# A fused attention, expert and softplus kernel: float64 conversion with one operand in PSUM, expert shares through ScalarE, input sums on GpSimd

## The chip, the cores and the metric

The kernel runs on one NeuronCore of a Trainium2 chip. The metric is the device time of one execution in microseconds (us); lower is better. Five engines work side by side, each with its own in-order queue: TensorE (PE, matrix products into PSUM), VectorE (DVE), ScalarE (ACT), GpSimd (POOL) and SyncE (SP), which only starts DMA transfers here. ACT starts a few transfers as well.

## The reference

Three stages follow each other. Shapes: q, k, v are (4, 8, 576, 64); the tokens that come out are 2304 rows of 512.

```
# 1 attention on keys and values averaged over groups of 8
k_p, v_p = mean of k, v over 8 neighbours           # 72 positions
x = softmax(q @ k_p.T / 8) @ v_p                    # -> x (2304, 512)
# 2 eight experts, every token goes to all of them
P = exp(x @ w_gate - max); 8 times: normalise rows, then columns; P *= N / E
out = sum over e of P[:, e] * (relu(x @ w1[e]) @ w2[e])   # w1 (8,512,1024)
# 3 softplus layer
out = softplus(out @ w_in) @ w_out                  # w_in (512,2048), w_out (2048,512)
```

The weights `w_in` and `w_out` of stage 3 arrive as float64, so the kernel has to turn 64-bit numbers into float32 on the chip, with integer operations on their two 32-bit words. All other inputs are float32.

## The kernel before

**Precision.** Each float32 product is done as three products of rounded halves: hi*hi, lo*hi, hi*lo, where hi is the value rounded to TensorE's format and lo the remainder. So every operand needs a `hi` (a copy by ACT) and a `lo` (a subtraction by POOL for weights, by DVE for most activations). `three` (line 791) issues the three matmuls.

**Phases and units.** The tokens are three groups ("pairs") of 768. `phases` (line 160) lists six phases: the expert layer on groups 0, 1, 2 (f = 0, 1, 2) and the softplus layer on groups 1, 2, 0 (f = 3, 4, 5). An expert phase has 32 units u (8 experts times 4 slices of 256 hidden columns), a softplus phase 8. A unit has a first part (x times w1, or w_in) and a second part (hidden times w2, or w_out). The list `todo` puts the first part of unit u+1 ahead of the second part of unit u.

**Fewer products.** The first part of every unit does a 2x2 block product with seven block products instead of eight; it needs four sums of input blocks, called t1 to t4, and remainders (lo) of the seven inputs, which are prepared during the phase before and parked in DRAM (`xlod`). In the two "block phases" f = 1 and 2 (`TWICE`) the second part is done the same way over pairs of units: the second part of an even unit has two form products, that of an odd unit has five, and the results are collected in seven matrices m1 to m7, which `joined` (line 1140) later adds up on POOL to the group's output.

**Side work.** What isn't part of the current unit is cut into small steps. `side` is a list of steps, with None for an empty slot; `hook` (line 1304) takes the next entry. Hooks stand between the products of a first part and after the tiles of a second part. If `side` is empty and the slot is marked light, `hook` calls `convert` instead. In the block phases hooks run in odd units only (`between`, line 1540); a chunk of conversion starts at k = 0 of an odd unit only if `side` is empty, and then goes on at each k. `ahead` (line 1484) fills `side` with the next phase's input sums and remainders: after unit 20 in f = 0, unit 2 in f = 1, unit 10 in f = 2. In f = 2 the seven joins of group 1 run by themselves from unit 0 on, two in each even unit (list `joins`).

**The conversion.** `from_float64` (line 1219) is a generator with six steps for each of 32 chunks of 128x512 numbers. `raw` holds a chunk's words in SBUF (tile `f`), `a` is a PSUM bank (`da`), `t` an SBUF tile (`dt`). Its DVE instructions stand on lines 1245, 1247, 1250, 1252, 1254, 1256 and 1257; line 1248 is one on ACT (absolute value). Line 1250 is the only one with both operands in SBUF:

```
ts(dn, dn, 1, None, op0=ALU.logical_shift_right)        # L1250: SBUF -> SBUF
```

In the same step as the last of them SP's store of the chunk (line 1258) and the load of the next chunk into the same raw buffer (line 1259) are issued. Two raw buffers exist until unit 26 of f = 0, one afterwards. `needed` forces chunks that a weight load is about to read.

**PSUM.** In f = 0 and the softplus phases there are four banks for first parts, three ("y") for second parts and one ("c") for side work. In the block phases PSUM is two sets (L, R) of double banks, each rotating by two.

**Shares.** In f = 0 the results of the first four experts are collected without their share P. Once P is known, `shares_to_raw` (line 1325) multiplies them in: for expert 0 one ACT instruction per tile, for the others one DVE instruction per tile that reads two SBUF tiles (line 1334), 18 in all.

Of the kernel before, what the change touches and what calls it, by code (L numbers as in the profile page):

```python
# [11 lines left out]
U32 = mybir.dt.uint32  # L12
# [7 lines left out]
def attention_moe_softplus_kernel(  # L20
# [637 lines left out]
    xs_next = {}  # L658
    spare = ["y"]

    def t_sums_banked(x, t):

        for o, a, b in (
            (t(0), block(x, 0, 1), block(x, 0, 0)), (t(2), block(x, 1, 1), block(x, 0, 1)),
            (t(1), block(x, 1, 1), t(0)), (t(3), block(x, 1, 0), t(1)),
        ):
            for c in range(2):
                got = []

                def copy(a=a, c=c, got=got):  # L670
                    got.append(bank("xs", spare[0])[:, :a.shape[2]])
                    nc.scalar.copy(got[0], a[:, c, :])

                def subtract(o=o, b=b, c=c, got=got):
                    nc.vector.tensor_tensor(o[:, c, :], got.pop(), b[:, c, :], op=ALU.subtract)

                yield copy
                yield subtract
# [67 lines left out]
    def sums_with_remainders(f, x, t, joins=()):  # L746

        parts = moe_parts(x, t)
        of = {name: q for q, (name, _) in enumerate(parts)}
        b = lambda i, j: block(x, i, j)  # L750
        ops = [
            *joins,
            (lambda: pool_sub(t(0), b(0, 1), b(0, 0)), "t1"),
            (lambda: pool_sub(t(2), b(1, 1), b(0, 1)), "t3"),
            (lambda: pool_sub(t(1), b(1, 1), t(0)), "t2"),
            (lambda: pool_sub(t(3), b(1, 0), t(1)), "t4"),
        ]
        ready = [] if joins else ["b11", "b21", "b22"]
        steps = []
        lag = [None, None]  # L760
        since = EVERY
        while ops or any(lag) or ready or steps:
            if (ops or any(lag)) and since >= EVERY:
                op, name = ops.pop(0) if ops else (None, None)
                lag.append(name)
                due = lag.pop(0)
                ready.extend([due] if due else [])
                since = 0
                if op:
                    yield op  # L770
                continue
            since += 1
            if not steps and ready:
                q = of[ready.pop(0)]
                steps = [*remainder(f, q, parts[q][1]), None]
            yield steps.pop(0) if steps else None
# [438 lines left out]

    f64_t = []
    converted = [0]

    def from_float64():

        ts, stt = nc.vector.tensor_scalar, nc.vector.scalar_tensor_tensor
        every = list(widths())
        unread = list(enumerate(every))
        loaded = []

        def fetch(at):
            if unread and at < len(f64_t):
                i, (src, _) = unread.pop(0)
                _, c, f, w = src.shape
                raw = f64_t[at].rearrange("p (c f w) -> p c f w", c=c, w=w)  # L1230
                nc.sync.dma_start(raw, src)
                loaded.append((i, at, raw))

        for at in range(len(f64_t)):
            fetch(at)
        for _ in range(4):
            yield True
        while loaded:
            i, at, raw = loaded.pop(0)
            up = raw[:, :, :, 1].rearrange("p c f -> p (c f)")  # L1240
            dn = raw[:, :, :, 0].rearrange("p c f -> p (c f)")
            size = lambda x: x.bitcast(F32)
            a = bank("da", "c", U32)
            t = tpool.tile([P, up.shape[1]], F32, tag="ex", name="dt")
            ts(a, up, 3, 0x3FFFFFF8, op0=ALU.logical_shift_left, op1=ALU.bitwise_and)
            yield False
            stt(a, up, 0xC0000000, a, op0=ALU.bitwise_and, op1=ALU.bitwise_or)
            nc.scalar.activation(size(up), size(up), AF.Abs)
            yield False
            ts(dn, dn, 1, None, op0=ALU.logical_shift_right)  # L1250
            yield False
            stt(t, size(up), 1.125 * 2.0 ** -15, size(a), op0=ALU.is_ge, op1=ALU.mult)
            yield False
            ts(a, t.bitcast(U32), 0xFF800000, None, op0=ALU.bitwise_and)
            yield False
            stt(size(a), dn, 2.0 ** -51, size(a), op0=ALU.mult, op1=ALU.mult)
            nc.vector.tensor_tensor(t, t, size(a), op=ALU.add)
            nc.sync.dma_start(every[i][1].rearrange("p c f -> p (c f)"), t)
            fetch(at)
            converted[0] += 1  # L1260
            yield True


    conversion = from_float64()
    between_chunks = [True]

    def convert():
        if converting[0] is not None:
            between_chunks[0] = next(conversion, None)
            if between_chunks[0] is None:  # L1270
                between_chunks[0] = True
                converting[0] = None

    def needed(chunks):
        while converted[0] < chunks:
# [49 lines left out]
    def shares_to_raw(experts):  # L1325

        for e in experts:
            for i in range(TP0 // P):
                def add(i=i, e=e):
                    a, s = acc_of(1, i), prob[:, i, e:e + 1]  # L1330
                    if e == 0:
                        nc.scalar.activation(a, a, AF.Copy, scale=s)
                    else:
                        nc.vector.scalar_tensor_tensor(a, raw_of(e, i), s, a, op0=ALU.mult, op1=ALU.add)
                side.extend([add, None, None] if e else [add])

    def load_x(pair):
        o = OFF[pair] - TP0
# [144 lines left out]

    def ahead(f, kind, u):

        if f + 1 == len(phases) or u != (20 if f == 0 else 10 if f == TWICE[-1] else 2 if kind == "moe" else 0):
            return
        nkind, npair = phases[f + 1]
        x, t = x_for(f + 1), t_in(t_at[f + 1], npair)
        if kind == "sp":  # L1490
            joins = ()
            if npair in TWICE:
                joins = joined(npair)
            else:
                for i in range(PAIRS[npair] // P):
                    side.extend([lambda i=i: turn(i, npair, 1), None])
            side.extend(sums_with_remainders(f + 1, x, t, joins))
            if joins:
                side.append(lambda: nc.sync.dma_start(g_t[1], gd))
            return  # L1500
        if nkind == "moe":
            side.append(lambda: load_x(npair))
            side.extend([None] * (8 if f == 0 else 5))
        if f == 0:
            for i, y in enumerate(t_sums_banked(x, t)):
                side.extend([y, None] if i % 2 else [y])
            for i, y in enumerate(remainders(f + 1, x, t)):
                side.extend([y, None] if i % 3 == 2 else [y])
            return
        side.extend(in_sixes(t_sums_banked(x, t), 2))  # L1510
        side.extend(in_sixes(remainders(f + 1, x, t), 3))

    joins = []

    for step, (what, n) in enumerate(todo):
# [3 lines left out]
        if what == "first":  # L1519
# [10 lines left out]
            if twice(n):  # L1530
                if not twice(n - 1):
                    while not between_chunks[0]:
                        convert()
                    open_banks("right", ("R", 2))
                    open_extra(
                        ("hhi", [P, 2 * TB], F32R), ("hlo", [P, 2 * TB], F32R), ("whi", [P, UC * HALF], F32R),
                        ("wlo", [P, UC * HALF], F32R), ("a21", [P, 2, TB], F32), ("s3", [P, 2, TB], F32),
                    )

                def between(k):  # L1540

                    if to_split and k in (1, 3, 4, 5):
                        to_split.pop(0)()
                    if u % 2 == 0:
                        if joins and k in (1, 4):
                            joins.pop(0)[0]()
                        return
                    if k == 0:
                        sharing[0] = not side
                    if not sharing[0]:  # L1550
                        hook()
                    elif k == 0 or not between_chunks[0]:
                        convert()

                away[0] = "LR"[u // 2 % 2]
# [36 lines left out]
        else:  # L1592
            if twice(n):
                second_twice(n)
                if f == TWICE[-1] and u == 0:
                    joins.extend(joined(TWICE[0]))
                if u == NU1 - 1 and not twice(n + 1):
                    assert not joins
                    open_extra(("xl", [P, 2 * TB], F32))
# [12 lines left out]
            for i in range(PAIRS[pair] // P):  # L1612
# [22 lines left out]
                    while more_stores:  # L1635
                        more_stores.pop(0)()
                if kind == "moe" or i >= 3:
                    hook(i >= (2 if f == 1 else 3))
            del h_t[n], w2_t[n]
            while pending:  # L1640
                pending.pop(0)()
# [43 lines left out]
```

## Time and profile before

| | us |
|---|---|
| median of 3 runs | 2017.49 |
| lowest and highest | 2008.28 and 2017.8 |
| the profiled execution's own time | 2014.24 |
| its span, first to last instruction | 2012.1 |

| engine | busy us | share of the span |
|---|---|---|
| PE (products) | 1953.7 | 97% |
| DVE | 1498.8 | 74% |
| POOL | 1472.0 | 73% |
| ACT | 971.0 | 48% |

The busy time of PE is modelled and its matmuls overlap, so a busy PE is not PE at its best pace. The chain that ended last is PE for 81% of the span and DVE for 9%. In a row of waits the first name is who waited, then for whom, then the total time, the number of waits and the longest. A row of the chain has a start, a length and what ran.

### The profile page before, as it was taken

The page shows a single profiled execution, that of the slowest core. Times are in us where ns is not written, and L with a number is a line of the kernel's source. Part 1 is how long each engine was busy: PE and PEld are TensorE (multiplying, and loading weights), DVE is VectorE, ACT ScalarE, POOL GpSimd, SP SyncE. Part 2 cuts the span into 40 slices and gives each one's busy share as a digit, 9 for nine tenths or more (in the row PEclk, how much of TensorE's full clock was granted, in tenths as well). Part 3 has the DMA queues.
Part 4 walks back from the last instruction along what each step waited for, and adds up shares of the span by engine and source line. Part 5 has one row for each costly group of instructions (what it writes and reads, how often), then busy time and mean ns, then how long its engine had stood idle before and what let it go on. Part 6 is the DMA issues. An engine that isn't in the chain of part 4 may idle for free.

```text
span 2012.1 us, 30503 instructions
## 1 busy us (share of the span) xinstructions
PE 1953.7 (97%) x10954; PEld 1804.6 (90%) x10954; DVE 1498.8 (74%) x2355; ACT 971.0 (48%) x1773; POOL 1472.0 (73%) x1134
## 2 busy tenths in 40 slices
PE   9899999999999999999999989999999989999999
PEld 7687788888988999999999889899999988888987
DVE  6775577887677777878888779888788866646455
ACT  6545334333334645554545544355554555655543
POOL 6776668777777777777777787677787868666553
PEclk9999999999999999999999999999999999999999
DMA  7444334555556654555555545444555532523411
GB/s 201 121 150 144 124 110 151 174 185 178 185 166 244 185 172 143 159 162 155 170 165 181 170 150 161 139 155 152 178 148 162 175 107 97 189 105 110 148 63 63
DMA packets 213347, 306.56 MB, mean 152 GB/s; under 512 B 33308, under 2 KB 147532, under 8 KB 212940
## 3 DMA queue, kind: packets, MB, share of 16 engines
q1 hardware_dynamic: 203116, 290.85, 45.9%
q10 hardware_dynamic: 10080, 13.77, 1.9%
q8 instruction: 86, 1.41, 0.3%
q14 instruction: 65, 0.53, 0.1%
HBM read 239.30 MB, written 65.27 MB: 151 GB/s over the span
## 4 chain that ended last, share of the span: by engine, by line
PE 81%; DVE 9%; POOL 3%; DMA 3%; issue 3%; ACT 1%; SPq 0%; DVEq 0%; ACTq 0%; POOLq 0%
PE py L794 42%; PE p L794 36%; DVE p L843 1%; DVE a L842 1%; POOL w1lo L289 1%; POOL w2lo L289 1%; DVE u L842 1%; PE px L522 1%; PE s L477 1%; PE pa L512 0%; DVE g L1126 0%; DMA xlod<-xl 0%; DMA f<-in_moe_w_out_dram 0%; DVE p L1039 0%; ACT w1hi L320 0%
## 5 line engine op out<-in xcount | busy, mean ns | idle before, releaser
L794 PE MATMUL p<-xhi,w1hi 128*128 128x384 f32 x1680 | 572.5, 341 | 19.6 <-DVE u L842 8.3
L794 PE MATMUL p<-xlo,w1hi 128*128 128x384 f32 x1680 | 565.1, 336 | 3.8 <-DMA xlo<-xlod 3.7
L794 PE MATMUL p<-xhi,w1lo 128*128 128x384 f32 x1680 | 565.8, 337 | 0.0
L289 POOL TENSOR_TENSOR w2lo<-w2raw,w2hi 128x512 fp32r<-128x512 f32 (+1 forms) x235 | 367.5, 1579 | 132.4 <-ACT w2hi L243 119.3
L289 POOL TENSOR_TENSOR w1lo<-w1raw,w1hi 128x512 fp32r<-128x512 f32 x240 | 239.6, 1021 | 248.4 <-ACT w1hi L320 248.3
L794 PEld LDWEIGHTS p<-xhi,w1hi 128*128 128x128 f32 x1680 | 316.5, 188 | 36.7 <-DVE u L842 9.2
L794 PEld LDWEIGHTS p<-xlo,w1hi 128*128 128x128 f32 x1680 | 316.8, 189 | 8.7 <-DMA xlo<-xlod 4.0
L794 PEld LDWEIGHTS p<-xhi,w1lo 128*128 128x128 f32 x1680 | 316.6, 188 | 0.0
L289 POOL TENSOR_TENSOR w1lo<-sums,w1hi 128x1024 fp32r<-128x1024 f32 x120 | 289.1, 2410 | 2.0 <-ACT w1hi L320 2.0
L794 PE MATMUL py<-w2hi,hhi 128*128 128x512 f32 x672 | 271.3, 404 | 9.0 <-DVE g L1126 7.2
L794 PE MATMUL py<-w2lo,hhi 128*128 128x512 f32 x672 | 266.3, 396 | 0.0
L794 PE MATMUL py<-w2hi,hlo 128*128 128x512 f32 x672 | 266.1, 396 | 0.0
L794 PE MATMUL py<-hhi,w2hi 128*128 128x384 f32 x716 | 245.8, 343 | 8.4 <-DVE a L842 8.4
L794 PE MATMUL py<-hhi,w2lo 128*128 128x384 f32 x716 | 242.1, 338 | 1.5 <-POOL w2lo L289 1.4
L794 PE MATMUL py<-hlo,w2hi 128*128 128x384 f32 x716 | 242.1, 338 | 0.0
L842 DVE TENSOR_TENSOR g<-py,g 128x768 f32<-128x768 f32 x210 | 199.7, 951 | 52.7 <-PE py L794 52.7
L886 ACT CAST hhi<-p 128x768 fp32r<-128x768 f32 x128 | 102.7, 802 | 249.3 <-DVE p L883 208.6
L794 PEld LDWEIGHTS py<-w2hi,hhi 128*128 128x128 f32 x672 | 126.7, 189 | 41.2 <-DVE g L1126 9.9
L794 PEld LDWEIGHTS py<-w2hi,hlo 128*128 128x128 f32 x672 | 126.6, 188 | 31.3
L794 PEld LDWEIGHTS py<-hhi,w2hi 128*128 128x128 f32 x716 | 135.3, 189 | 19.2 <-DVE a L842 16.1
L794 PEld LDWEIGHTS py<-w2lo,hhi 128*128 128x128 f32 x672 | 127.0, 189 | 24.4
L794 PEld LDWEIGHTS py<-hhi,w2lo 128*128 128x128 f32 x716 | 135.3, 189 | 2.4 <-POOL w2lo L289 2.4
(161 smaller groups left out, 3565.1 us busy)
## 6 DMA issues: line engine op xcount, KB each, us to landing
w1raw<-in_moe_w_dram SPq DMA_DIRECT2D x96, 512.0 KB
w2raw<-td SPq DMA_DIRECT2D x128, 256.0 KB
sums<-sd SPq DMA_DIRECT2D x62, 512.0 KB
w2raw<-in_moe_w_dram SPq DMA_DIRECT2D x96, 256.0 KB
w2raw<-in_moe_w_dram SPq DMA_DIRECT2D x32, 512.0 KB
sd<-sums SPq DMA_DIRECT2D x32, 512.0 KB
td<-w2raw SPq DMA_DIRECT2D x64, 256.0 KB
xlo<-xlod SPq DMA_DIRECT2D x35, 384.0 KB
```

Of the source, the lines that this page charges most:

```text
L289: nc.gpsimd.tensor_tensor(o, a, b, op=ALU.subtract)
L477: nc.tensor.matmul(ps[:QP, j * 2 * SP:(j + 1) * 2 * SP], qT[:, j * QP:(j + 1) * QP], kb)
L522: nc.tensor.matmul(px[h * D:(h + 1) * D, :W], vp[:, h, :], aT[:, h, :])
L794: nc.tensor.matmul(ps, lhs[a], rhs[b], start=first and i == 0, stop=last and i == 2, skip_group_check=goes_on,)
L842: vadd = lambda o, x, y: nc.vector.tensor_tensor(o, x, y, op=ALU.add)
L843: vsub = lambda o, x, y: nc.vector.tensor_tensor(o, x, y, op=ALU.subtract)
L886: nc.scalar.copy(h_slot(q)[0], src)
```

## The change

Four things change.

1. Conversion. The bank `a` takes over what `t` held and the other way round, and the shift of the low word (line 1250) no longer works in place in SBUF but writes to a PSUM bank `r`: in the block phases the second half of the same double bank, elsewhere a bank from the three of the second part. Every DVE instruction of a chunk now has exactly one operand in PSUM (or reads SBUF and writes PSUM).
2. Store and next load of a chunk are put off (`settle`): in the block phases to k = 2 of the following even unit; elsewhere to the next call of `convert`, after which 3 calls (two raw buffers) or 10 calls (one buffer) pass before the next chunk starts. No chunk starts in unit 31 of a block phase. In f = 0 the third tile of a second part becomes a light slot too.
3. Shares. For experts 1 to 3 ACT scales the raw tile into a "y" bank and, a hook later, DVE adds that bank to the sum.
4. Input sums of the phases 2 and 3 (f + 1 when f is 1 or 2) are done by four POOL instructions of 128x768 instead of sixteen steps by ACT and DVE through a bank. They run from unit 0 on in even units, at k = 1 and 4, behind `load_x` (f = 1) or the seven joins (f = 2); then `side` gets the remainders.

```diff
+    def t_sums(x, t):
+        b = lambda i, j: block(x, i, j)
+        return [
+            (lambda: pool_sub(t(0), b(0, 1), b(0, 0)), "t1"),
+            (lambda: pool_sub(t(2), b(1, 1), b(0, 1)), "t3"),
+            (lambda: pool_sub(t(1), b(1, 1), t(0)), "t2"),
+            (lambda: pool_sub(t(3), b(1, 0), t(1)), "t4"),
+        ]
...
-            a = bank("da", "c", U32)
+            in_c = "c" in banks
+            if in_c:
+                a = bank("da", "c", U32)
+            else:
+                both = banks[away[0]].tile([P, 2, 512], U32, tag=f"two{away[0]}", name="da")
+                a, r = both[:, 0], both[:, 1]
...
-            ts(dn, dn, 1, None, op0=ALU.logical_shift_right)
+            if not in_c:
+                ts(r, dn, 1, None, op0=ALU.logical_shift_right)
             yield False
-            stt(t, size(up), 1.125 * 2.0 ** -15, size(a), op0=ALU.is_ge, op1=ALU.mult)
+            stt(size(a), size(up), 1.125 * 2.0 ** -15, size(a), op0=ALU.is_ge, op1=ALU.mult)
             yield False
-            ts(a, t.bitcast(U32), 0xFF800000, None, op0=ALU.bitwise_and)
+            ts(t.bitcast(U32), a, 0xFF800000, None, op0=ALU.bitwise_and)
             yield False
-            stt(size(a), dn, 2.0 ** -51, size(a), op0=ALU.mult, op1=ALU.mult)
-            nc.vector.tensor_tensor(t, t, size(a), op=ALU.add)
-            nc.sync.dma_start(every[i][1].rearrange("p c f -> p (c f)"), t)
-            fetch(at)
-            converted[0] += 1
+            if in_c:
+                r = bank("dr", "y", U32)
+                ts(r, dn, 1, None, op0=ALU.logical_shift_right)
+            stt(t, r, 2.0 ** -51, t, op0=ALU.mult, op1=ALU.mult)
+            nc.vector.tensor_tensor(t, size(a), t, op=ALU.add)
+            def done(i=i, at=at, t=t):
+                nc.sync.dma_start(every[i][1].rearrange("p c f -> p (c f)"), t)
+                fetch(at)
+                converted[0] += 1
+            settle.append(done)
             yield True
...
     def convert():
-        if converting[0] is not None:
+        if pause[0]:
+            pause[0] -= 1
+            settled()
+        elif converting[0] is not None:
+            settled()
             between_chunks[0] = next(conversion, None)
             if between_chunks[0] is None:
                 between_chunks[0] = True
                 converting[0] = None
+            elif settle:
+                pause[0] = PAUSE[len(f64_t)]
+    PAUSE = {2: 3, 1: 10}
...
+                def scaled(i=i, e=e, got=got):
                     a, s = acc_of(1, i), prob[:, i, e:e + 1]
-                    if e == 0:
-                        nc.scalar.activation(a, a, AF.Copy, scale=s)
-                    else:
-                        nc.vector.scalar_tensor_tensor(a, raw_of(e, i), s, a, op0=ALU.mult, op1=ALU.add)
+                    if e:
+                        got.append(bank("ra"))
+                    nc.scalar.activation(got[0] if e else a, raw_of(e, i), AF.Copy, scale=s)
+                def add(i=i, got=got):
+                    a = acc_of(1, i)
+                    nc.vector.tensor_tensor(a, got.pop(), a, op=ALU.add)
...
-        side.extend(in_sixes(t_sums_banked(x, t), 2))
-        side.extend(in_sixes(remainders(f + 1, x, t), 3))
+        if nkind == "moe":
+            joins.append(lambda: load_x(npair))
+            joins.extend([lambda: None] * 3)
+        else:
+            joins.extend(op for op, _ in joined(npair))
+        joins.extend(op for op, _ in t_sums(x, t))
+        joins.extend([lambda: None] * 2)
+        joins.append(lambda: side.extend(in_sixes(remainders(f + 1, x, t), 3)))
...
                     if u % 2 == 0:
+                        if k == 2:
+                            settled()
                         if joins and k in (1, 4):
-                            joins.pop(0)[0]()
+                            joins.pop(0)()
                         return
                     if k == 0:
                         sharing[0] = not side
+                        pause[0] = 0
                     if not sharing[0]:
                         hook()
-                    elif k == 0 or not between_chunks[0]:
+                    elif (k == 0 and u < NU1 - 1) or not between_chunks[0]:
                         convert()
...
-                    hook(i >= (2 if f == 1 else 3))
+                    hook(i >= 2)
```

## Rows read from the trace of the kernel before

**Rows 1.** The page, busy time of the engines: us, share of the span, instructions.
```profile
PE 1953.7 (97%) x10954; PEld 1804.6 (90%) x10954; DVE 1498.8 (74%) x2355; ACT 971.0 (48%) x1773; POOL 1472.0 (73%) x1134
```

**Rows 2.** Waits of PE: for whom, us in total, times, longest us.
```profile
PE p L794 <- DVE u L842: 8.3, 2, 4.5
PE p L794 <- DVE p L1039: 7.4, 2, 6.1
PE py L794 <- DVE g L1126: 7.2, 5, 3.2
PE p L794 <- DMA xlo<-xlod: 3.7, 1, 3.7
...
PE p L794 <- DVE g L842: 1.1, 1, 1.1
```

**Rows 3.** The chain that ended last: start us, length us, what ran.
```profile
349.70 6.27 PE p L794 x36
...
485.43 6.26 PE p L794 x36
...
501.13 6.26 PE p L794 x36
...
806.12 4.17 PE p L794 x24
...
836.01 4.20 PE p L794 x24
...
1047.17 4.35 PE p L794 x24
...
1077.41 4.34 PE p L794 x24
...
1142.79 4.47 PE p L794 x24
...
1307.58 4.34 PE p L794 x24
...
1643.32 8.28 PE py L794 x30
...
1660.32 7.00 PE py L794 x30
```

**Rows 4.** Busy time by stretch: us, PE, PEld, DVE, ACT, POOL, PEclk, DMA, GB/s.
```profile
400.00:450.00 50.00, 47.13 (x230) 41.42 (x229) 44.25 (x70) 16.29 (x30) 36.16 (x30) 0.98 0.55 170
...
1142.80:1307.60 164.80, 153.27 (x841) 148.53 (x842) 139.91 (x174) 76.39 (x121) 127.55 (x87) 0.98 0.49 149
```

**Rows 5.** Conversion lines 1250 and 1245: duration ns min/median/max, first and last start.
```profile
L1250 DVE TENSOR_SCALAR f<-f x32: 419/424/7006, 366.1 to 1641.3; 128x512 uint32<-128x512 uint32 x32
...
L1245 DVE TENSOR_SCALAR da<-f x32: 682/684/696, 363.3 to 1638.5; 128x512 uint32<-128x512 uint32 x32
```

**Rows 6.** DVE in order of time: start, length, what; in brackets idle before it.
```profile
1195.31 7.01 DVE L1250 TENSOR_SCALAR f<-f 128x512 uint32<-128x512 uint32 x1
```

**Rows 7.** POOL in order of time, the same stretch.
```profile
1199.65 2.38 POOL L289 TENSOR_TENSOR w1lo<-sums,w1hi 128x1024 fp32r<-128x1024 f32 x1
```

**Rows 8.** Groups of DVE and of POOL instructions: busy us, mean ns, idle before.
```profile
L1334 DVE SCALAR_TENSOR_TENSOR g<-g,prob,g 128x512 f32<-128x512 f32 x18 | 23.8, 1324 | 0.0
...
L286 POOL TENSOR_TENSOR g<-g,g 128x768 f32<-128x768 f32 x8 | 14.7, 1848 | 0.2
```

**Rows 9.** Waits of all engines between 380 and 400 us.
```profile
ACT f L1248 <- DVE da L1247: 7.6, 2, 6.1
```

**Rows 10.** DVE in order of time, a quiet chunk around 1098 us.
```profile
1100.21 0.56 DVE L842 TENSOR_TENSOR u<-p,za 128x384 f32<-128x384 f32 x1 [1.64 <-PE p L794]
```

**Rows 11.** SP's DMA issues in order of time at the end of phase 1.
```profile
1105.21 0.32 SPq L1258 DMA_DIRECT2D v<-dt  x1
...
1107.44 1.84 SPq L685 DMA_DIRECT2D xlo<-xlod  x3
```

**Rows 12.** DVE in order of time, phase 3, unit 1.
```profile
1638.49 0.69 DVE L1245 TENSOR_SCALAR da<-f 128x512 uint32<-128x512 uint32 x1 [4.49 <-DMA f<-in_moe_w_out_dram]
```

More of the change, by code (lines that the diff above doesn't have):

```diff
@@ L749, in sums_with_remainders @@
         of = {name: q for q, (name, _) in enumerate(parts)}
[L750 to L757, printed above, removed]
+        ops = [*joins, *t_sums(x, t)]
         ready = [] if joins else ["b11", "b21", "b22"]
@@ L1217, in attention_moe_softplus_kernel @@
     converted = [0]
+    settle = []
+    pause = [0]
     def from_float64():
@@ L1265, in attention_moe_softplus_kernel, with settled @@
     between_chunks = [True]
+    def settled():
+        while settle:
+            settle.pop(0)()
     def convert():
-        if converting[0] is not None:
+        if pause[0]:
[3 more added lines that the diff above has]
+            settled()
             between_chunks[0] = next(conversion, None)
@@ L1328, in shares_to_raw @@
             for i in range(TP0 // P):
-                def add(i=i, e=e):
+                got = []
+                def scaled(i=i, e=e, got=got):
                     a, s = acc_of(1, i), prob[:, i, e:e + 1]
-                    if e == 0:
-                        nc.scalar.activation(a, a, AF.Copy, scale=s)
-                    else:
-                        nc.vector.scalar_tensor_tensor(a, raw_of(e, i), s, a, op0=ALU.mult, op1=ALU.add)
-                side.extend([add, None, None] if e else [add])
+                    if e:
[4 more added lines that the diff above has]
+                    nc.vector.tensor_tensor(a, got.pop(), a, op=ALU.add)
+                side.extend([scaled, add, None] if e else [scaled])
     def load_x(pair):
@@ L1484, in ahead @@
     def ahead(f, kind, u):
-        if f + 1 == len(phases) or u != (20 if f == 0 else 10 if f == TWICE[-1] else 2 if kind == "moe" else 0):
+        if f + 1 == len(phases) or u != (20 if f == 0 else 0):
             return
@@ L1490, in ahead @@
         if kind == "sp":
-            joins = ()
+            joins_of = ()
             if npair in TWICE:
-                joins = joined(npair)
+                joins_of = joined(npair)
             else:
@@ L1496, in ahead @@
                     side.extend([lambda i=i: turn(i, npair, 1), None])
-            side.extend(sums_with_remainders(f + 1, x, t, joins))
-            if joins:
+            side.extend(sums_with_remainders(f + 1, x, t, joins_of))
+            if joins_of:
                 side.append(lambda: nc.sync.dma_start(g_t[1], gd))
             return
-        if nkind == "moe":
+        if f == 0:
             side.append(lambda: load_x(npair))
-            side.extend([None] * (8 if f == 0 else 5))
-        if f == 0:
+            side.extend([None] * 8)
             for i, y in enumerate(t_sums_banked(x, t)):
@@ L1544, in between @@
                     if u % 2 == 0:
+                        if k == 2:
+                            settled()
                         if joins and k in (1, 4):
-                            joins.pop(0)[0]()
+                            joins.pop(0)()
                         return
@@ L1594, in attention_moe_softplus_kernel @@
                 second_twice(n)
-                if f == TWICE[-1] and u == 0:
-                    joins.extend(joined(TWICE[0]))
                 if u == NU1 - 1 and not twice(n + 1):
```

## The prediction

> **What bounds the kernel now.** I read the page first. PE is busy for 97% of the span [rows 1], so the change, which leaves all its products as they are, can only win what PE loses somewhere. Where it loses is read from the chain of waits [rows 3]: the start of the same product in successive units gives the pace. In phase 0 a unit takes 501.13 - 485.43 = 15.70 us. In a block phase a pair of units takes 836.01 - 806.12 = 29.89 us without a conversion chunk and 1077.41 - 1047.17 = 30.24 us with one, so a chunk costs 0.35 us there. Against these paces four stretches stand out:
>
> - 349.70 to 485.43 (phase 0, eight units): 135.73 - 8 x 15.70 = 10.1 us too long.
> - 1077.41 to 1142.79 (phase 1 to 2, two pairs): 65.38 - 60.48 = 4.9 us.
> - 1142.79 to 1307.58 (phase 2, five pairs, with the joins): 164.79 - 151.20 = 13.6 us.
> - phase 3, unit 1: PE waits 6.1 us for the DVE sum on line 1039 [rows 2], and the next 30 matmuls take 8.28 instead of 7.00 us [rows 3], together 7.4 us.
>
> With a wait of 1.1 us for DVE at the end of phase 2 [rows 2] that is 37 us, the most that there is to win. The waits of PE [rows 2] name DVE in all but one, a DMA (3.7 us). So the question in each stretch is what held DVE.
>
> **The change part by part.** Times are set against the profiled execution: span 2012.1 us, its own time 2014.24. The median of the three runs shown is 3.3 us higher, and they lie 9.5 us apart; I take my sum as the median after.
>
> *Shift into PSUM, phase 2 (-11.6).* Line 1250 has a median of 424 ns and a longest of 7006 ns [rows 5]. That longest one starts at 1195.31 [rows 6] and lasts until 1202.32, just behind the end of a train of POOL instructions at 1199.65 + 2.38 = 1202.03 [rows 7]: DVE got its turn only when POOL paused. PE's two waits for line 842 (8.3 us, [rows 2]) are this one and one like it. The stretch was also granted 0.98 of the clock [rows 4], 2% of 164.8 = 3.3 us. That leaves 13.6 - 8.3 - 3.3 = 2.0 for the joins themselves. The changed line reads SBUF and writes PSUM, as line 1245 does, and that one took 682 to 696 ns in all 32 chunks [rows 5], the same crowded stretch among them. So both waits and the slow clock behind them go: 8.3 + 3.3 = 11.6, between 0 (if the wait stays) and 13.6.
> The Trainium skill (SBUF - State Buffer, Who interferes with whom) says that a DVE instruction with at most one SBUF input and outside its two-port modes does not contend with GpSimd, which line 1245 bears out. It also says that the loser is held for the other's whole instruction, which would be 2.38 us here; the 7.0 us of the trace are longer, and the trace decides.
>
> *Its price elsewhere (0).* In quiet chunks the line goes from 424 to 684 ns, +0.26 us on DVE. Lowest 0; highest, all on the path, 22 chunks in the block phases x 0.26 = 5.7. I take 0: right behind this line DVE idles for 1.64 us until PE's product arrives [rows 10], which hides it.
> The Trainium skill (VectorE: DVE Perf Modes, Why PSUM operands drop a tier) speaks against the change here: an fp32 operation that reads or writes PSUM loses the double rate. The rows agree on the price; were it all exposed, the sum would be 5.7 higher.
>
> *Load of the next chunk, phase 3 (-7.4, +1.0).* DVE stood 4.49 us for the raw words [rows 12], because the load was issued only with the end of the chunk before and the next chunk began at once. Now ten calls pass; a call comes about twice in a product of 1.04 us (6.26 us for 36 matmuls, [rows 3]), so the pause is 5 us or more, longer than the wait. All 7.4 go. By my count of the hooks two chunks still fall into phase 3. They cost something between 0 and the present 7.4; I take 1.0, since their data will have landed.
>
> *No chunk in unit 31, store later (-3.0, -1.1).* At the end of phase 1 SP's queue held the store behind DVE until 1105.21; behind it stand the next load, two weight loads and at 1107.44 the last three remainders (xlo) [rows 11], for which PE waits 3.7 us [rows 2]. Gone are a store of 256 KB and a load of 512 KB. The least this gives is the queue's time for them, some 0.9 us; 786 KB at the 170 GB/s of [rows 4] would be 4.6 us, more than the wait. I take 3.0, nearer to the upper end. At the end of phase 2 the wait of 1.1 us for DVE goes, since the chunk's last steps stood ahead of that sum on DVE.
>
> *Pauses and shares, phase 0 (-7.0).* Per unit there were 7 + 3 = 10 light slots and 6 steps per chunk, 1.67 chunks; now 11 slots and 6 + 3 calls, 1.22 chunks. With 6 x 0.684 + 0.424 = 4.53 us of DVE per chunk before and 7 x 0.684 = 4.79 after, DVE falls from 7.6 to 5.8 us per unit, or from 44.25 to 38.5 us in the stretch of 50 [rows 4]. Of the shares, 18 DVE instructions fall from 1324 ns [rows 8] to about 690 (the length of line 1245, [rows 5]). What stalled PE was a DVE queue so long that ACT, in order, stood 6.1 us for a conversion step [rows 9] with the relu behind it; PE then waited 7.2 us in five waits for the sums on line 1126 [rows 2], plus slow clock. With DVE under 80% this should mostly go: -7.0, between 0 and -10.1.
>
> *More chunks in the block phases (+1.1).* From the hooks: 9 + 10 chunks before, 11 + 11 after (side work ends sooner in units 1 to 11 and 1 to 13, none in unit 31), three more at 0.35.
>
> *Input sums on POOL (+2.9).* What they replace ran in pairs of 29.89 us, so it cost PE nothing. Eight POOL instructions of 1848 ns [rows 8] are added: between 0 and 14.8 us. The nearest case is the joins: three even units with two POOL additions each left 2.0 us, 0.67 per unit; 4.3 such units are added (two in phase 1, the rest in phase 2).
>
> *Drain into phase 1 (+1.0).* The eighth chunk is half done when phase 0 ends, and its last three steps (5 DVE instructions, 3.4 us) are issued at once ahead of phase 1. Between 0 and 3.4, as DVE has room there.
>
> *Banks (+1.5).* The shares (18) and the chunks of phase 0 (8) take turns in the three "y" banks. While one is in it, PE may run only one tile ahead of DVE. Between 0 and 26 x 1.4 (one tile, 7.00 / 5, [rows 3]) = 36 us. I take 1.5, since seven of thirteen hooks of a unit lie in the first part, which uses no y bank, and DVE is less loaded.
>
> Sum: -11.6 - 7.4 - 3.0 - 1.1 - 7.0 = -30.1; +1.0 + 1.1 + 2.9 + 1.0 + 1.5 = +7.5. 2014.2 - 22.6 = 1991.6, say 1992 us.
>
> **The rivals.**
>
> - *Phase 0 keeps its stalls.* DVE still has 38 of 50 us there and ACT still waits in order for it. Without the 7.0 the time is 1999.
> - *POOL becomes the bound in the block phases.* It is busy for 127.55 of 164.8 us in the stretch with the joins [rows 4] and would get 1.85 us for each further sum. If all 14.8 us show, the time is 1992 + 11.9 = 2004. Against it: 77% leaves room for 3.7 us more in a pair of 30.
> - *The shift's price shows.* If DVE's 1.64 us are used up by other delays, 5.7 us more: 1997.
> - *The change does not free DVE.* If something else than the shared port held line 1250, the 11.6 stay: 2003. Line 1245's 696 ns speak against it.
> - *The y banks, slower.* In phase 0 each of the 26 uses holds up PE for a full tile of 1.4 us: 1992 + 34.9 = 2027. From 0.93 us per use (24.1 / 26) the change wins nothing. For it: DVE runs late in second parts [rows 9]; against it: with three banks PE waits there only when DVE is several us behind.
> - *All waits go and nothing new comes:* 2014 - 37 + 1 = 1978.
>
> **How the numbers follow.** Forecast 0.45, phase 0 keeps its stalls 0.17, the shift's price 0.08, POOL 0.11, no freeing 0.05, y banks 0.07, all waits gone 0.07. A measurement can tell about 0.5%, 10 us, from no change, so faster means under 2007. Forecast, phase 0, price and the best case lie well below it (0.77); POOL and no freeing lie just below, and half of them counts as faster (0.08), the other half as the same, with a little of the y banks, which lie at the upper edge. Faster 0.85, the same 0.09, slower 0.06. The range runs from 1979, near the best case, to 2006, which takes in the POOL case and leaves out the y banks.
>
> **What will show it.** Right: no DVE instruction of the conversion over 0.75 us; pairs of 30.2 to 31 us all through the first half of phase 2; no DVE wait on the raw words in phase 3; the wait for xlo under 1 us. Wrong: PE waiting for w2lo or w1lo of POOL between 690 and 900 us and between 1140 and 1330 us; PE waiting for the share sums or for "dr" between 300 and 480 us; a pair with a chunk over 30.5 us. If phase 0 from unit 15 to 23 still takes over 132 us, the term of 7.0 was wrong.

## The result and the profile after

| | before | changed |
|---|---|---|
| median, us | 2017.64 (4 runs) | 1991.34 (4 runs) |
| lowest and highest, us | 2008.28 and 2019.16 | 1990.21 and 1996.32 |
| profiled execution, own time, us | 2014.24 | 1996.32 |
| its span, us | 2012.1 | 1994.5 |

The ratio is 0.9884, 95% interval 0.985 to 0.9918. It was measured once more beside other kernels: 0.9883, 0.9855 to 0.9911. The forecast was 1992 us. A run more than 1.5% above the fastest of its kernel is left out of ratios and comparisons; here that is one, of the kernel with the shift back in SBUF.

The page of the changed kernel, busy time of the engines, answers to [rows 1]: PE does the same work, DVE does 28 us less.

```profile
PE 1955.4 (98%) x10954; PEld 1802.7 (90%) x10954; DVE 1470.4 (74%) x2339; ACT 977.7 (49%) x1777; POOL 1476.8 (74%) x1142
```

The waits of PE in the changed kernel (for whom, total us, times, longest) answer to [rows 2].

```profile
PE py L797 <- DVE a L845: 10.4, 30, 0.4
PE py L797 <- POOL w2lo L289: 3.1, 5, 0.7
PE p L797 <- DVE p L1042: 2.3, 3, 1.3
PE py L797 <- DVE g L1129: 1.9, 4, 1.2
...
PE p L797 <- DMA xlo<-xlod: 1.6, 1, 1.6
...
PE p L797 <- ACT whi L243: 1.1, 1, 1.1
```

The wait of 8.3 us for DVE's line 842 is gone from the list, the one for the sum of line 1039 (now 1042) fell from 7.4 to 2.3 us, the one for the sums of line 1126 (now 1129) from 7.2 to 1.9. The first row, 30 waits of at most 0.4 us, is the same in the kernel before (10.5 us, line 842). The waits for GpSimd's w2lo, now second, were 1.4 us in two waits before.

The chain of the changed kernel (start us, length, what ran) at the places of [rows 3]:

```profile
355.73 6.26 PE p L797 x36
...
484.38 6.26 PE p L797 x36
...
1048.30 4.37 PE p L797 x24
...
1078.56 4.36 PE p L797 x24
...
1140.09 4.47 PE p L797 x24
...
1295.59 4.36 PE p L797 x24
```

Read as before: eight units of phase 0 take 128.7 us (before 135.7); a pair with a chunk 30.26 (30.24); the two pairs around the change from phase 1 to 2, 61.5 (65.4); the five pairs with the joins 155.5 (164.8).

PE's granted clock answers to [rows 4]. Before, PE waited 2.9, 3.7, 4.5, 3.7 and 6.1 us at five places, and around the end of each wait or just behind it there is a stretch at 0.50 of the clock, the 1.2 GHz level (columns as in [rows 4]; a wait of 3.2 us in unit 17 of phase 0 has none behind it):

```profile
447.94:451.36 3.42, 3.42 (x9) 2.34 (x8) 3.33 (x6) 1.77 (x4) 3.42 (x3) 0.50 0.65 204
1116.95:1120.37 3.42, 3.42 (x12) 3.42 (x11) 1.59 (x3) 0.02 (x1) 3.42 (x4) 0.50 0.63 161
1202.29:1205.70 3.41, 2.86 (x9) 2.86 (x10) 2.32 (x5) 0.00 (x0) 0.00 (x0) 0.50 0.02 5
1270.55:1273.97 3.42, 3.42 (x13) 3.42 (x12) 3.23 (x7) 0.00 (x0) 0.00 (x0) 0.50 0.00 0
1639.19:1646.02 6.83, 4.99 (x13) 4.41 (x14) 6.12 (x11) 5.87 (x10) 2.40 (x3) 0.50 0.09 37
```

The changed kernel has full clock from 90 us on, to within 1 us of its end:

```profile
90.20:1994.00 1903.80, 1875.94 (x10199) 1737.69 (x10197) 1407.87 (x2203) 926.10 (x1633) 1420.47 (x1076) 1.00 0.47 154
```

The five stretches last 20.5 us together. At half the clock they cost about 10 us (an estimate from these rows), so a good part of the gain is the clock that PE no longer loses behind its waits.

A finer reading takes the first product of each unit's first part and subtracts successive starts. This gives a time for each unit that repeats within some hundredths of a us from kernel to kernel where nothing was changed, except in the first three units, in units 9 and 20 of phase 1, in unit 0 of phase 2 and where PE stalls: the kernel *No joins* below is the kernel before up to phase 2, and takes 107.0 us in units 16 to 21 of phase 0, where the kernel before took 104.3. So the differences of phase 0 hold to about 3 us. From the fourth unit on, all in which the kernel before and the changed one differ by 0.3 us or more:

| phase, unit | before | changed | difference |
|---|---|---|---|
| 0, 13 and 14 | 15.71, 16.06 | 16.46, 15.72 | +0.4 |
| 0, 17 | 20.10 | 16.92 | -3.2 |
| 0, 19 | 15.71 | 17.31 | +1.6 |
| 0, 20 and 21 | 20.61, 16.41 | 15.82, 15.72 | -5.5 |
| 0, 29 | 16.29 | 15.72 | -0.6 |
| 1, 6 and 8 | 18.39, 18.44 | 19.41, 19.39 | +2.0 |
| 1, 9 | 11.52 | 11.88 | +0.4 |
| 1, 20 | 18.84 | 18.37 | -0.5 |
| 2, 0 | 23.34 | 19.65 | -3.7 |
| 2, 5 and 9 | 17.59, 17.09 | 11.78, 11.76 | -11.1 |
| 2, 8 and 10 | 18.45, 18.40 | 19.42, 19.42 | +2.0 |
| 3, 1 | 24.36 | 16.51 | -7.9 |
| 3, 2 | 15.72 | 17.30 | +1.6 |

With the differences under 0.3 us the units from the fourth on sum to -23.5 us (the last unit, which no other follows, is 0.3 us longer up to the end of the span). The profiled execution of the changed kernel had lost 5.6 us by the end of its third unit, 4.9 of them ahead of the first, where the change does nothing; in the second measurement that start was 0.3 us shorter than before, and the span was 1988.3 us, 23.8 less than before.

The shift of the low word, in the block phases and elsewhere (duration ns min/median/max), answers to [rows 5]: no instance is long any more.

```profile
L1261 DVE TENSOR_SCALAR da<-f x22: 694/695/697, 644.9 to 1557.0; 128x512 uint32<-128x512 uint32 x22
...
L1269 DVE TENSOR_SCALAR dr<-f x10: 682/684/689, 374.1 to 1637.0; 128x512 uint32<-128x512 uint32 x10
```

### The profile page after: what moved, and what is told of

Its sections match the earlier page's. It is cut to its first block, busy times and chain, and to the rows that moved or that the text cites. A ratio compares the mean times of both kernels' runs of the same rounds, so it can differ in the third digit from the quotient of the medians.

```text
span 1994.5 us, 30491 instructions
## 1 busy us (share of the span) xinstructions
PE 1955.4 (98%) x10954; PEld 1802.7 (90%) x10954; DVE 1470.4 (74%) x2339; ACT 977.7 (49%) x1777; POOL 1476.8 (74%) x1142
## 4 chain that ended last, share of the span: by engine, by line
PE 79%; POOL 7%; DVE 6%; issue 4%; ACT 2%; DMA 2%; SPq 0%; ACTq 0%; POOLq 0%; DVEq 0%
PE py L797 40%; PE p L797 36%; POOL w1lo L289 3%; POOL w2lo L289 1%; DVE p L846 1%; DVE a L845 1%; PE s L477 1%; PE px L522 1%; POOL g L289 1%; DVE u L845 1%; POOL hlo L893 1%; PE pa L512 1%; ACT w1hi L320 1%; DVE p L1042 0%; DMA qt<-in_q_dram 0%
## 5 line engine op out<-in xcount | busy, mean ns | idle before, releaser
L797 PEld LDWEIGHTS py<-w2hi,hlo 128*128 128x128 f32 x672 | 126.2, 188 | 31.2
```

What stands on the lines that cost most here:

```text
L797: nc.tensor.matmul(ps, lhs[a], rhs[b], start=first and i == 0, stop=last and i == 2, skip_group_check=goes_on,)
```

## Experiments

Unit times below are read as in the table. Kernels that ran once are compared by units. The edits are shown in part; `...` and comments behind `#` are added.

**Shift back in SBUF** (changed kernel, arithmetic of a chunk as before):

```diff
-                ts(r, dn, 1, None, op0=ALU.logical_shift_right)      # r in PSUM
+            ts(dn, dn, 1, None, op0=ALU.logical_shift_right)         # in place
...
```

> The changed kernel with the arithmetic of a chunk as before (the shift in place, SBUF to SBUF), all else as changed. Port theory: DVE gets the shared port only when GpSimd pauses, so the line takes 0.42 us in quiet chunks and several us where GpSimd runs without a gap; the two waits of 6 to 7 us in phase 2 come back (+11 us) and, as GpSimd now has its sums in phase 1 units 6 to 9 and phase 2 units 8 to 11 too, perhaps more: 2002 to 2012 us. Rival, the later store and load or the fewer chunks freed DVE, not the operand: 1990 us, and no such line over 1.5 us.

Ratio to the kernel before 1.0025 (1.0 to 1.005): the whole gain is lost and more than was expected. Unit 7 of phase 1 takes 18.31 us and units 7, 9 and 11 of phase 2 take 18.95, 18.69 and 18.59, all 11.8 in the changed kernel: 27.5 us more in these four. The line's four long instances last 7.00 to 7.03 us. One of them on DVE, and POOL at the same time:

```profile
1224.49 7.03 DVE L1255 TENSOR_SCALAR f<-f 128x512 uint32<-128x512 uint32 x1
```

```profile
1221.95 3.82 POOL L289 TENSOR_TENSOR w2lo<-w2raw,w2hi 128x512 fp32r<-128x512 f32 x3
1225.71 1.32 POOL L289 TENSOR_TENSOR wlo<-w2raw,whi 128x512 fp32r<-128x512 f32 x1
1226.96 1.98 POOL L289 TENSOR_TENSOR w1lo<-w1raw,w1hi 128x512 fp32r<-128x512 f32 x2
1228.87 2.37 POOL L289 TENSOR_TENSOR w1lo<-sums,w1hi 128x1024 fp32r<-128x1024 f32 x1
```

DVE's instruction ends at 1231.52, just behind the end of POOL's train at 1231.24. Each instruction of the train starts as the one before ends, and DVE's instruction ends only when the train is over. The Trainium skill (SBUF - State Buffer, Who interferes with whom) has the loser blocked for one instruction of the other; here it was five.

**New operands alone** (kernel before, with the chunk's arithmetic of the change and nothing else of it):

```diff
+                both = banks[away[0]].tile([P, 2, 512], U32, tag=f"two{away[0]}", name="da")
+                a, r = both[:, 0], both[:, 1]
...
-            ts(dn, dn, 1, None, op0=ALU.logical_shift_right)
+                ts(r, dn, 1, None, op0=ALU.logical_shift_right)
...
```

> The kernel before with the new operands of a chunk alone (store, load, shares and sums as before). Port theory: units 5 and 9 of phase 2 fall from 17.6 and 17.1 to 11.8 us, 11 us less than before in all, ratio about 0.994 to 0.995, with the stalls of phase 0 (units 17 and 20) and of phase 3 (unit 1, 24 us) still there. Rival, the operand does not matter: ratio 1.000.

Ratio 0.9973 (0.9955 to 0.999), half of the gain that was expected. Units 5 and 9 of phase 2 take 11.76 and 11.77 us: the 11 us are there. But units 16 to 21 of phase 0 take 107.7 us instead of 104.3, which was not expected. There the chunks follow each other without pause, and the new bank of each is taken from the three that PE writes its second parts to. That this costs the 3.4 us is not shown: *No joins*, with the old operands, takes 107.0 in the same units.

**Input sums on ScalarE and DVE** (changed kernel with the sums through a bank, at the old units):

```diff
-        joins.extend(op for op, _ in t_sums(x, t))
+        side.extend(in_sixes(t_sums_banked(x, t), 2))
...
```

> The changed kernel with the input sums of the block phases on ScalarE and DVE through a bank again, at their old units. Theory that each even unit with two GpSimd additions costs about 1.0 us because the second stands ahead of w1lo and w2lo in GpSimd's queue: units 6 and 8 of phase 1 and 8 and 10 of phase 2 fall from 19.4 to 18.4 us, 4 us; but side work lasts longer there, so about 5 chunks move out of the block phases into phase 3, where one cost about 1.2 us: net 1986 to 1993 us. Rival, the sums cost nothing on GpSimd and the 19.4 us come from the chunks: no change in these units.

Ratio 1.0052 (1.0034 to 1.0071), slower than before. Units 6 and 8 of phase 1 and 8 and 10 of phase 2 fall to 18.37 to 18.51 us as the first theory said, but the side work of the sums keeps odd units occupied, and seven chunks are left for phase 3 instead of two. Its units 5 and 6 take 33.3 and 33.2 us: a weight load forces the rest, one chunk after the other, and each waits for its words. First PE's waits, then DVE in order of time (in brackets the idle time before):

```profile
PE py L797 <- DVE dt L1270: 26.2, 4, 7.0
```

```profile
1693.68 0.70 DVE L1255 TENSOR_SCALAR da<-f 128x512 uint32<-128x512 uint32 x1 [4.22 <-DMA f<-in_moe_w_in_dram]
```

So what the sums on GpSimd bring is not their own time, which was hidden before, but five odd units for chunks. The expectation had priced the chunks that move at 1.2 us each and had not seen that forced ones wait for their loads.

**Sums and joins one to an even unit** (at k = 1; two in unit 2 of phase 2):

```diff
+        for q, op in enumerate(ops):        # ops: joins and sums, two: 0 or 2
+            joins.append(op)
+            if q >= two:
+                joins.append(rest_in)       # an empty slot
...
```

> The changed kernel with the same GpSimd sums and joins one to an even unit (at k = 1 alone; two in unit 2 of phase 2), so phase 1 needs units 6 to 12 and phase 2 units 2 to 20. Queue theory: an addition at k = 1 has room, the one at k = 4 delays w2lo; five units with two additions fall from 19.4 to 18.5 us and five or six units with one gain less than 0.1 each: 4 to 5 us less, 1986 us. Rival, GpSimd is short of time as a whole and every addition costs about 0.5 us wherever it stands: no gain, 1991 us.

Ratio 0.9867 (0.9841 to 0.9892), with an interval that overlaps that of the changed kernel. Of the six units at 19.4 us five fall to between 18.46 and 18.52, unit 4 of phase 2 to 18.80, and a sum that stands alone costs about 0.1 us or less. POOL in the changed kernel around the wait in unit 6 of phase 1, then PE:

```profile
725.02 1.85 POOL L289 TENSOR_TENSOR g<-g 128x768 f32<-128x768 f32 x1
726.82 2.01 POOL L289 TENSOR_TENSOR w1lo<-w1raw,w1hi 128x512 fp32r<-128x512 f32 x2
728.77 2.44 POOL L289 TENSOR_TENSOR w1lo<-sums,w1hi 128x1024 fp32r<-128x1024 f32 x1
731.13 1.31 POOL L289 TENSOR_TENSOR w2lo<-w2raw,w2hi 128x512 fp32r<-128x512 f32 x1
```

```profile
732.50 0.45 PE L797 MATMUL py<-hhi,w2lo 128*128 128x384 f32 x1 [0.68 <-POOL w2lo L289]
```

The sum at k = 4 stands ahead of w1lo and of the w2lo that PE needs next. It is not POOL's load as a whole that costs 1 us, since the same number of additions is done. The trace points to the place in the queue; a single addition at k = 4 was not tried. Unit 0 of phase 2 took 21.72 us here, see the last experiment.

**No pause in phase 0** (changed kernel):

```diff
-    PAUSE = {2: 3, 1: 10}
+    PAUSE = {2: 0, 1: 10}
```

> The changed kernel without the pause of three calls in phase 0 (with one raw buffer the ten calls stay). Density theory: chunks come every 6 slots instead of 9, DVE's queue grows past what ScalarE's in-order wait and PE's banks can take, and the stalls of units 16 to 21 return: 7 to 12 us more in phase 0 than the changed kernel, as in the kernel with the new operands alone; two or three chunks more are done there, so phase 3 has none and gains 2.4 us. Rival, the phase-0 gain came from the shares on ScalarE: phase 0 within 2 us of the changed kernel.

One run, 1997.83 us. Units 16 to 22 take 118.0 instead of 112.9 us: the pause is worth 5.0, less than the 7 to 12 expected. Units 1 and 2 of phase 3, without chunks now, take 15.72 and 15.71, 2.4 less, as expected.

**Shares on DVE** (changed kernel):

```diff
-                    nc.scalar.activation(got[0] if e else a, raw_of(e, i), AF.Copy, scale=s)
+                        nc.vector.scalar_tensor_tensor(a, raw_of(e, i), s, a, op0=ALU.mult, op1=ALU.add)
...
```

> The changed kernel with the shares on DVE as before (two SBUF inputs). Port theory: some of these 18 instructions take 2 to 3 us again; units 10 to 15 lose what the bank costs (unit 13 from 16.46 to 15.71, unit 14 from 15.72 to 16.06), and unit 17 rises by 1 to 3 us from 16.9, since the last six shares stand ahead of its sums: 1 to 3 us slower than the changed kernel in phase 0. Rival, the pauses alone cured phase 0 and the shares matter for nothing: within 0.5 us.

One run, 1995.58 us. Unit 13 falls to 15.71, unit 14 rises to 16.06, unit 17 to 17.91, unit 19 to 17.50: 0.8 us in all, between the two theories. The line is stretched as before (ns min/median/max; 734/989/2770 in the kernel before), but most of that is hidden:

```profile
L1364 DVE SCALAR_TENSOR_TENSOR g<-g,prob,g x18: 736/986/2810, 314.0 to 416.8; 128x512 f32<-128x512 f32 x18
```

**Absolute value one step later** (changed kernel, ScalarE's step behind the shift):

```diff
-            nc.scalar.activation(size(up), size(up), AF.Abs)
             yield False
             if not in_c:
                 ts(r, dn, 1, None, op0=ALU.logical_shift_right)
+            nc.scalar.activation(size(up), size(up), AF.Abs)
```

> The changed kernel with ScalarE's absolute value of a chunk issued one step later, behind the shift. Theory that what is left in phase 0 (units 17 and 19, 1.2 and 1.6 us) is ScalarE standing in order for a DVE step that is itself late, with the relu behind it: these two units fall by 1 us or more each, and unit 2 of phase 3 by some of its 1.6 us. Rival, what is left is the y bank that a chunk takes: units 17 and 19 stay at 16.9 and 17.3 us.

One run, 1990.55 us. Units 17 and 19 take 16.83 and 17.37 us, and unit 2 of phase 3 stays at 17.30: the theory of ScalarE's in-order wait falls for what is left there.

**No pause with one raw buffer** (changed kernel):

```diff
-    PAUSE = {2: 3, 1: 10}
+    PAUSE = {2: 3, 1: 0}
```

> The changed kernel with no pause where there is one raw buffer (10 to 0). By a count of the hooks two chunks move from phase 3 to the end of phase 0, where units 28 to 31 had none. Theory that a chunk in phase 3 costs PE 1 us or more because ScalarE and DVE have the softplus there: units 1 and 2 of phase 3 fall to 15.7 us (2.4 us less), the end of phase 0 rises by less than 1 us. Rival, the two units of phase 3 are slow after the change of phase whatever the chunks: they stay at 16.5 and 17.3 us. If a chunk meets its raw words too early at the end of phase 0, units 29 to 31 show a wait of up to 5 us for the load.

One run, 1999.71 us. Phase 3 falls by 2.4 us as expected, and the two chunks meet their words too early: unit 29 and 31 of phase 0 and unit 0 of phase 1 rise by 0.7, 6.3 and 1.2 us. DVE:

```profile
613.41 0.69 DVE L1255 TENSOR_SCALAR da<-f 128x512 uint32<-128x512 uint32 x1 [3.96 <-DMA f<-in_moe_w_in_dram]
```

That is the stall of [rows 12], made anew at another place by taking the pause away.

**Spread sums, old operands in phases 0 and 3:**

```diff
+            ts(dn if in_c else r, dn, 1, None, op0=ALU.logical_shift_right)
+            whole, part = (t, size(a)) if in_c else (size(a), t)
...
+            stt(part, dn if in_c else r, 2.0 ** -51, part, op0=ALU.mult, op1=ALU.mult)
```

> The changed kernel with two edits that the runs so far point to: GpSimd's sums and joins one to an even unit, and the old operands (shift in place in SBUF) wherever a chunk uses the single bank 'c', that is in phase 0 and phase 3, the new ones in the block phases. Bank theory: in phase 0 the extra bank of a chunk, taken from the three of the second parts, costs unit 19 its 1.6 us (it took 15.8 with the shift in SBUF); unit 17 stays at 16.9. Sums: 5 us less in the block phases. 6 to 7 us faster than the changed kernel run beside it, ratio to the kernel before about 0.985. Rival: the old shift meets GpSimd's trains in phase 0 and gives the 1.6 us back; 5 us faster then.

> The changed kernel itself, beside the one above on the same chip: 1990 to 1996 us, ratio 0.988, units 17 and 19 of phase 0 at 16.9 and 17.3 us, four units of 19.4 us in the block phases that the other kernel has at 18.5.

The combination has 1986.64 us, ratio 0.9846 (0.9818 to 0.9874), the changed kernel beside it 1992.22 us, ratio 0.9883 (0.9855 to 0.9911): the fastest version, though the intervals still overlap. By units it gains 1.65 us in phase 0 (unit 19 from 17.30 to 15.79) and 6.2 in the block phases, and lost 3.0 in unit 0 of phase 2. The gain beside the changed kernel, 5.6 us by the medians, was expected at 6 to 7.

**No joins** (kernel before, the seven GpSimd additions of phase 2 left out):

```diff
-                    joins.extend(joined(TWICE[0]))
+                    joins.extend([(lambda: None, None)] * 7)
```

> The kernel before, with the seven additions on GpSimd left out that join group 1's matrices in phase 2 (so what follows from them is not the reference's). Port theory: without them GpSimd has pauses, line 1250 finds its turn within 2 us, and units 4 to 9 of phase 2 fall to 18.4 and 11.8 us: 13 to 14 us less. Rival, line 1250 is long because of something else at that place (a late raw chunk, a semaphore, the bank): the two waits of 6 to 7 us stay, and only the 2 us of late w2lo go.

One run, 2004.58 us. Units 5 and 9 of phase 2 take 11.75 us each, units 4 and 6, 18.44 and 18.52; the seven units 4 to 10 take 13.1 us less. Nothing of the conversion was changed, and its line has no long instance (ns min/median/max):

```profile
L1250 DVE TENSOR_SCALAR f<-f x32: 419/421/1998, 366.4 to 1631.8; 128x512 uint32<-128x512 uint32 x32
```

**Chunk in unit 31** (changed kernel):

```diff
-                    elif (k == 0 and u < NU1 - 1) or not between_chunks[0]:
+                    elif k == 0 or not between_chunks[0]:
```

> The changed kernel with a chunk in unit 31 of the block phases again; its store and next load still wait for the next even unit. Queue theory: what held the last remainders in phase 1 to 2 was the store and the load ahead of them in SP's queue and in the DMA engines; put off, they hold up nothing, and unit 0 of phase 2 stays near 19 to 20 us (up to 21.8, as it varies from run to run). Rival, the chunk itself (DVE late, so the slots of xlo late) made the wait: unit 0 goes back to 23.3 us. One or two chunks fewer remain for phase 3, 1.2 us each.

One run, 1991.42 us. Unit 0 of phase 2 took 22.34 us. In the ten profiles without that chunk it took 18.97 to 22.11 us, in the three that store at once 23.34 to 24.42. It lies between the theories, and how much is the chunk and how much the store and load stays open. What unit 0 gains varies by 3 us among kernels without the chunk; why is not shown. Phase 3, with no chunk left, takes 2.4 us less, so over all units this kernel and the changed one are within 0.2 us.

## Why the prediction was right

*Shift into PSUM, phase 2:* -11.6 predicted, -11.3 measured (units 5, 7 and 9). Both halves of the term are there: PE's two waits of 8.3 us, and the two stretches at half clock behind them, 6.8 us long, so about 3.4 lost (3.3 predicted). The cause is shown from both sides: the two waits go with the operands alone changed, and also with the operands kept and POOL's additions gone; with the additions kept and the operand put back, waits of this kind return. What the prediction did not see: the sums that the change adds on POOL would have made four such waits, 27.5 us, had the operand stayed. The two parts need each other.

*Its price elsewhere:* 0 predicted, 0 measured. The line takes 695 ns instead of 424, and a pair with a chunk 30.26 us instead of 30.24.

*Load of the next chunk, phase 3:* -6.4 net predicted, -6.3 measured. The two halves were both too small: the old stall was 8.6 us (the prediction counted the slow clock on 30 products only, the six ahead of them ran slow too), and the two chunks cost 2.4 instead of 1.0 us. The prediction expected only their data to matter. But each of these chunks brings two loads of the table that ACT computes its functions from (ACT_TABLE_LOAD), as its absolute value stands between softplus activations. ACT in the changed kernel between 1600 and 1650 us, then in the kernel of *Chunk in unit 31*, which has no chunk there:

```profile
1604.01 1.28 ACT L817 ACT_TABLE_LOAD   x1
1617.13 1.28 ACT L1258 ACT_TABLE_LOAD   x1
1619.12 1.28 ACT L817 ACT_TABLE_LOAD   x1
1633.63 1.28 ACT L1258 ACT_TABLE_LOAD   x1
1641.48 1.28 ACT L817 ACT_TABLE_LOAD   x1 [1.80 <-DVE xl L741]
```

```profile
1601.66 1.28 ACT L817 ACT_TABLE_LOAD   x1
```

How much of the 2.4 us the four further loads make was not separated from the chunks' other work.

*Unit 31:* -3.0 predicted for the change from phase 1 to 2, -3.7 measured, in the second measurement -4.2. By the spread of unit 0 (18.97 to 22.11 us without the chunk, 23.34 to 24.42 where it is stored at once) it could have been anything from -1.2 to -5.5, so it is luck that the size came out. The 1.1 us at the end of phase 2 were wrong: unit 31 falls by 0.1 us, from 12.95 to 12.83. The wait is still there, now put down to ACT's whi. DVE's sum, which ends when PE goes on, starts with the product it waits for and has nothing ahead of it, before and after:

```profile
1608.12 0.96 DVE L842 TENSOR_TENSOR g<-py,g 128x768 f32<-128x768 f32 x1 [0.25 <-PE py L794]
```

```profile
1596.40 0.96 DVE L845 TENSOR_TENSOR g<-py,g 128x768 f32<-128x768 f32 x1 [0.67 <-PE py L797]
```

So the prediction had put a chunk into a chain that it wasn't in.

*Pauses, shares and banks, phase 0:* -7.0 + 1.5 = -5.5 predicted, -7.2 measured for units 13 to 29; set against the phase 0 of *No joins*, which is that of the kernel before, it would be -10.2. The pauses give 5.0 and the shares 0.8, each by one run. Unit 19 loses 1.5 that go with the old operands, by the bank or by the later place of the shift. Unit 13 loses 0.7 that go with the shares on DVE, by the bank or by ACT's instruction; this is in the 0.8 already. These parts make 4.3 of the 7.2; the rest has no run of its own (the later store, the third light slot). The slower rival, that the banks cost PE a full tile at each use, is refuted: 1.5 and 0.7 us are far from its 36. What is left in unit 17, 1.2 us, was not explained.

The path that the prediction gave, ACT standing in order for a conversion step and the relu behind it, is not shown. In units 15 to 22 ACT's waits for that step are as long in the mean after as before (4.7 and 4.9 us), only fewer, while PE's waits for the sums nearly went. First the kernel before, then the changed one:

```profile
ACT f L1248 <- DVE da L1247: 44.0, 9, 8.0
...
PE py L794 <- DVE g L1126: 6.7, 3, 3.2
```

```profile
ACT f L1258 <- DVE da L1257: 33.2, 7, 6.7
...
PE py L797 <- DVE g L1129: 1.4, 2, 1.2
```

*Input sums on POOL:* +2.9 predicted, +4.0 measured. The unit price was mis-sized: 0.67 was a mean over three units with joins that cost 0.40, 0.98 and 0.83 us (set against *No joins*); the four units with sums cost 0.95 to 1.02. The prediction read PE's waits as waits for DVE in all but one, and passed over POOL's w2lo, which stood among them with 1.4 us in two waits. The POOL rival, in which POOL's load is the bound, is refuted by spreading the same additions.

*More chunks:* +1.1 predicted, +0.7 measured. *Drain:* +1.0 predicted, 0 measured: unit 0 of phase 1 takes 15.84 us instead of 15.82.

Of the signs that the prediction named, three of being wrong came: PE waits for w2lo (3.1 us, before 1.4), six pairs with a chunk take 31.2 to 31.3 us, and the wait for xlo is 1.6 us (1.1 in the second measurement) instead of under 1. The first two are the sums and joins on POOL. The signs for the shift (no conversion instruction over 0.75 us), the raw words and phase 0 (128.7 us, under 132) came out right.

The sum, -22.6 predicted against -23.5, is nearer than its terms; errors of both signs of up to 1.7 us cancelled. And that the median came out at 1991.34 for 1992 is luck in part: the sum was counted from the profiled execution of the kernel before, 3.4 us under its median. From median to median the change gives -26.3 us, in the second measurement -27.2.

## What to carry to other kernels

When one engine is busy for 97%, list the pace of its units and work only on those that fall out of it; here nearly all of the gain was in eight of 120. A wait can cost more than its length: behind five of them PE went on at half its clock. An instruction that waits for a busy engine can look cheap by its median and is to be judged by its maximum: here 424 ns against 7 us. And where two engines trade work, the place of an added instruction in its queue, and the slots that it frees elsewhere, counted more than its own length.

## What was not expected of the hardware

DVE's wait for the port lasted whole trains of POOL instructions: four waits of 7.00 to 7.03 us, against 2.4 us for the longest POOL instruction in them. With the shift in SBUF and all sums on POOL eleven runs spread from 2002.54 to 2029.02 us, while five runs of the changed kernel lie within 1990.11 to 1997.9 us. That it is a matter of luck which engine comes first would explain this, but it is not shown: of the eleven one was traced.
